# Attention and a wave mixer on one core: gates five loads deep, v copies on VectorE, x of batch 1 transposed by TensorE, padded v rows, a new issue order

## The chip, the cores and the metric

One core of one Trainium2 chip runs the whole program. The metric is the time of one execution in microseconds on the device, the median over runs. The span of a profile, from the first to the last instruction, is 1.7 to 1.8 us shorter than the time of the same execution. Only ratios from runs beside each other on one chip are compared closely.

## The reference, cut to what matters

```python
# q, k, v: (4 batches, 8 heads, 768, 64); each query sees 96 local keys and 8 global ones
scores = scale * q @ k^T + bias          # bias: -slope(head) * distance
a = softmax(where(keep, scores, -1e9))
x = (a @ v) as (4, 768, 512)
theta = x @ w_theta
y = w_tok_r @ (x * cos(theta)) + w_tok_i @ (x * sin(theta))   # over the 768 tokens
u = x + y
out = u + max(u @ w_ch, 0)
```

The kernel takes float32 inputs and computes in bf16. Each batch passes through attention in three groups `g` of 256 rows. The names in the profile are the tiles: `qk` (loaded q and k), `vn` (loaded v with a column of ones), `vp` (a copy of `vn` whose first 8 rows are the global rows), `e` (exponentials), `x`, `xT`, `zri` (x·cos, x·sin), `w_tokT`, `u`, `uT`.

## The kernel before

Every instruction is a named operation, issued in the order of one long string. Nothing is scheduled at run time: each engine takes its instructions in that order. The engine times and latencies handed to `add` are ignored here (`add` drops them), so the numbers in them change nothing on the chip.

```python
class Plan:
    def add(self, name, eng, fn, **_):
        op = self.ops[name] = SimpleNamespace(name=name, fn=fn, took=next(iter(eng)))
    def issue(self, order):              # "q000/DVE" sets the engine, then issues
        ...
DEPTH = 3
v_bufs  = [const.tile([T, 2, H, D + 1], BF, ...) for i in range(NV)]
vp_bufs = [const.tile([T, 2, H, D + 1], BF, ...) for i in range(NV)]

def load(fn, us, ndesc, spot, depth=0, ...):     # fn issues one DMA from GpSimd
    ...
    if depth:        # loads 24 to 86: a tiny GpSimd copy that reads load n-depth
        add(f"gate{n}", ..., lambda: nc.gpsimd.tensor_copy(out=scrap, in_=landed[n - depth]()), ...)
    add(f"load{n}", ..., fn, ...)

def vprev(b, g):     # vp: v with the global rows put in rows 0..7
    if b == 0:       # two VectorE copies, vpa and vpb
        ...
    else:            # two DMAs on the SP queue
        add(f"vpa{b}{g}", {"SP": 0.88}, lambda: nc.sync.dma_start(out=dst[NG:T], in_=src[NG:T]), ...)
        add(f"vpb{b}{g}", {"SP": 0.76}, lambda: nc.sync.dma_start(out=dst[0:NG]..., in_=first...), ...)

def xtrans(b, g):
    if b == 0:       # 8 TensorE transposes, then one copy xc out of PSUM
        ...
    else:            # one DMA transpose on the SP queue
        ...
```

A gate makes GpSimd wait until the load three places back has landed. So three of the gated loads are in flight at most. A q, k or v load moves 256 KB of float32 from HBM as 1024 pieces of 64 numbers.

The softmax here doesn't subtract the row's maximum and nothing guards it: scores larger than these inputs give would overflow.

Of the kernel before, what the change touches and what calls it, by code (L numbers as in the profile page):

```python
# [10 lines left out]
BF = mybir.dt.bfloat16  # L11
# [25 lines left out]
ones5 ones1 ones6 halfpi ones2 zero load1 ones3 ones0 ones4 warm0 load2 load3 rel load4 sid6 far0 sid2 far1  # L37
load5 dtab0 sid4 dtab1 dtab2 sid0 load6 sid3 sid1 sid5 sid7 ident dtab3 load7 t0001 etab6 bi0000 bi0001 bi0010
bi0011 etab3 load8 t0000 t0010 q000/DVE t0011 q001/ACT k000/DVE load9 k001/ACT kg000 load10 etab0 kg001 s001
etab5 load11 s000 t0100 x0000 load12 t0110 x0001 q010/DVE bi0020 x0010 bi0021 k010/DVE load13 s002 x0011  # L40
bi0030 etab1 bi0031 s003 load14 x0020 kg010 vpa00 x0021 bi0100 vpb00 load15 etab4 bi0101 s010 etab2 v002
load16 v000 v001 x0100 n000 x0101 load17 t0200 n002 x0030 q020/DVE x0031 load18 t0210 etab7 n001 bi0110 v003
load19 bi0111 k020/DVE s011 bi0120 load20 x0110 bi0121 s012 kg020 x0111 load21 n003 bi0130 x0120 vpa01 bi0131
load22 s013 x0121 vpb01 bi0200 load23 vpa02 x0130 xt00 vpb02 bi0201 x0131 v010 xc00/DVE v012 v013 n010 s020
v011 n012 x0200 bi0210 bi0211 n011 s021 x0201 bi0220 n013 x0210 bi0221 s022 x0211 xt01 x0220 gate24 bi0230
xc01/DVE bi0231 load24 x0221 v020 s023 n020 th000 gate25 x0230 load25 x0231 th010 cos000 gate26 load26 v023
th011 n023 gate27 v022 load27 sin000 tw11 n022 tw10 tw01 twc11/DVE gate28 twc10/ACT v021 load28 z000 th001
twc01/ACT n021 gate29 tw00 load29 cos001 xt02 twc00/DVE sin001 xc02/DVE cos010 gate30 load30 z001 sin010 th021
# [42 lines left out]
def kernel(  # L91
# [25 lines left out]

    bufs = dict(qk=6, qT=3, kk=3, e=8, x=8, xT=3, zri=5, cs=3, u=4, uT=3, o=3, w_nat=9, pa=4, pb=4)
# [4 lines left out]
    add = plan.add  # L123
    tiles = {}
# [531 lines left out]
```

## Time and profile before

| | before |
|---|---|
| time, median of 3 (range) | 204.88 us (203.74 to 206.62) |
| span of the profiled run | 203.4 us |
| TensorE busy | 172.8 us |
| VectorE / ScalarE busy | 127.2 / 100.1 us |
| TensorE idle in gaps over 0.15 us | 25.2 us |
| last load (86) lands at | 149.9 us |

The profiled run took 205.13 us and is labelled slow, which on one core only says that it is over 1.5% above the fastest run known of this kernel.

First, the page: busy time, and the span in 40 slices, where a digit is the busy share in tenths, and for `PEclk` the granted clock.

```profile
span 203.4 us, 3971 instructions
...
PE 172.8 (85%) x1532; PEld 91.7 (45%) x1532; DVE 127.2 (63%) x280; ACT 100.1 (49%) x175; POOL 84.9 (42%) x154
...
PE   7589789897949958898846998949999999999990
...
PEclk9999969999996999999987999997999999999997
```

TensorE (PE) is full in the last third and full of holes before it. The 6s and 7s of the clock row are windows of 3.4 us at half clock, four of them before the tail. The Trainium skill, "TensorE: Matmul & The Clock Gate", part 1, says that TensorE's clock is halved after an idle window of about 3.4 us and restored after a busy one; the trace agrees on the length of the windows (3.4 us each). What counts as idle it leaves open: TensorE's longest idle stretch in this run is 3.0 us, and the window at 27 us begins after a gap of 1.7 us.

The list of waits shows what ended TensorE's gaps: total us, times, longest.

```profile
PE pb L303 <- DMA w_nat<-in_moe_w_tok_r_dram: 5.7, 3, 2.5
PE pb L321 <- DMA qk<-in_q_dram: 5.6, 3, 2.6
PE pa L483 <- DMA xT<-x: 4.7, 3, 3.0
PE pb L321 <- DMA qk<-in_k_dram: 2.2, 2, 1.8
...
PE pa L440 <- DMA vp<-vn: 0.9, 2, 0.5
```

And what GpSimd (POOL) waited for in its gates, from the same view:

```profile
POOL scrap L207 <- DMA qk<-in_k_dram: 16.6, 13, 3.0
POOL scrap L207 <- DMA vn<-in_v_dram: 10.2, 9, 2.1
POOL scrap L207 <- DMA w_nat<-in_moe_w_tok_i_dram: 8.0, 2, 7.1
POOL scrap L207 <- DMA w_nat<-in_moe_w_tok_r_dram: 5.6, 3, 3.0
POOL scrap L207 <- DMA qk<-in_q_dram: 4.9, 8, 1.2
```

`scrap` is the output of a gate. The chain of waits (start, length, what) puts the two together; the gates and issues between these lines, under 1 us each, are left out:

```profile
69.36 6.00 DMA w_nat<-in_moe_w_tok_r_dram
75.95 3.68 DMA vn<-in_v_dram
80.20 5.15 DMA qk<-in_k_dram
85.92 5.57 DMA vn<-in_v_dram
92.06 6.19 DMA qk<-in_k_dram
98.82 3.57 DMA vn<-in_v_dram
...
104.35 7.18 DMA qk<-in_k_dram
111.57 0.40 PE pb L321 x4
```

Between 69 and 111 us the end of the program hangs on loads, each issued only when the one three back had landed.

### The profile page before, as it was taken

Reading aid. Unit: us, or ns where it says so; the run is one execution under the profiler, and the core shown is the slowest. Engines: PE = TensorE matmul, PEld = TensorE weight load, DVE = VectorE, ACT = ScalarE, POOL = GpSimd, SP = SyncE. Lnnn points to the kernel's source line nnn. Section 1 sums busy time; section 2 is a strip of 40 time slices with the busy share of each in tenths; the row PEclk is TensorE's granted clock in tenths of the full one; section 3 lists DMA queues with packets and bytes.
Section 4 is the critical chain, followed back from the end, with each engine's and each line's share of the span. In section 5 each row is a group of like instructions: output and inputs, shape, how many; then the busy total and the mean of one; then the engine's idle time right before and its main releaser. Section 6 shows DMA issues by size and latency. Waiting matters only on the chain.

```text
span 203.4 us, 3971 instructions
## 1 busy us (share of the span) xinstructions
PE 172.8 (85%) x1532; PEld 91.7 (45%) x1532; DVE 127.2 (63%) x280; ACT 100.1 (49%) x175; POOL 84.9 (42%) x154
## 2 busy tenths in 40 slices
PE   7589789897949958898846998949999999999990
PEld 1355446543624635534432554416464554444440
DVE  2467664875833857674643899525999786453341
ACT  2389748894204609566820777517944574210010
POOL 7999136624636537656562834536400000000000
PEclk9999969999996999999987999997999999999997
DMA  5999979998999999999999999999978375413433
GB/s 38 117 134 152 161 129 99 111 145 129 95 130 128 182 172 113 171 83 210 108 130 113 109 156 197 137 183 152 156 124 141 104 131 130 130 60 69 159 72 135
DMA packets 101323, 26.39 MB, mean 130 GB/s; under 512 B 94447, under 2 KB 97151, under 8 KB 101303
## 3 DMA queue, kind: packets, MB, share of 16 engines
q0 software_dynamic: 77664, 12.85, 87.0%
q1 hardware_dynamic: 23639, 13.28, 30.7%
q8 instruction: 12, 0.20, 0.4%
q14 instruction: 8, 0.07, 0.1%
HBM read 25.69 MB, written 6.29 MB: 157 GB/s over the span
## 4 chain that ended last, share of the span: by engine, by line
DMA 41%; PE 40%; POOL 11%; issue 4%; ACT 1%; DVE 0%; POOLq 0%
PE pb L525 19%; DMA qk<-in_k_dram 9%; PE pb L565 8%; DMA w_nat<-in_moe_w_tok_r_dram 8%; DMA vn<-in_v_dram 6%; POOL qk L220 6%; DMA xT<-x 6%; PE pa L483 5%; DMA w_nat<-in_moe_w_tok_i_dram 4%; DMA qk<-in_q_dram 4%; DMA w_ch_bf<-in_moe_w_ch_dram 4%; PE pa L388 3%; POOL vn L234 3%; PE pa L440 2%; PE pb L321 2%
## 5 line engine op out<-in xcount | busy, mean ns | idle before, releaser
L525 PE MATMUL pb<-zri,w_tokT 128*128 128x512 bf16 x288 | 71.8, 389 | 0.0
L411 ACT ACTIVATE e<-pa 128x512 bf16<-128x512 f32 (+1 forms) x96 | 46.7, 570 | 36.3 <-PE pa L388 36.0
L525 PEld LDWEIGHTS <-w_tokT 128*128 128x128 bf16 x288 | 26.7, 100 | 29.4 <-issue 2.8
L483 PE MATMUL pa<-w_theta_bf,xT 128*128 128x512 bf16 x96 | 24.6, 393 | 5.5 <-DMA xT<-x 4.7
L492 ACT ACTIVATE cs<-pa,halfpi 128x512 bf16<-128x512 f32 x24 | 16.6, 690 | 20.2 <-PE pa L483 20.2
L419 DVE TENSOR_TENSOR e<-e,etab 128x1024 bf16<-128x1024 bf16 (+1 forms) x36 | 22.4, 640 | 5.5 <-ACT e L411 5.5
L537 DVE TENSOR_TENSOR u<-x,pb 128x512 bf16<-128x512 bf16 x24 | 16.4, 684 | 13.6 <-PE pb L525 13.6
L565 PE MATMUL pb<-w_ch_bf,uT 128*128 128x512 bf16 x96 | 24.5, 380 | 0.0
L321 PE MATMUL pb<-ident,qk 128*128 128x128 bf16 x192 | 17.2, 243 | 8.1 <-DMA qk<-in_q_dram 5.6
L220 POOL DMA_DIRECT2D qk<-in_k_dram x24 | 22.1, 921 | 3.2 <-issue 2.9
L234 POOL DMA_DIRECT2D vn<-in_v_dram x24 | 21.2, 896 | 4.1 <-issue 4.1
L220 POOL DMA_DIRECT2D qk<-in_q_dram x24 | 21.3, 889 | 3.4 <-issue 2.0
L388 PE MATMUL pa<-qT,kk 64*128 64x128 bf16 x352 | 18.8, 230 | 2.0 <-ACT e L411 0.8
L504 DVE TENSOR_TENSOR zri<-x,cs 128x1024 bf16<-128x1024 bf16 x24 | 16.3, 686 | 6.5 <-ACT cs L494 6.3
L572 DVE SCALAR_TENSOR_TENSOR o<-pb,u 128x512 f32<-128x512 f32 x24 | 16.5, 686 | 5.9 <-PE pb L565 5.9
L321 PEld LDWEIGHTS <-qk 128*128 128x128 bf16 x192 | 14.1, 110 | 13.3 <-DMA qk<-in_q_dram 7.1
L440 PEld LDWEIGHTS <-e 128*128 128x128 bf16 x352 | 14.7, 98 | 9.1 <-issue 2.2
L333 DVE COPY kk<-pb 128x2048 bf16<-128x2048 bf16 (+1 forms) x12 | 14.1, 1175 | 7.1 <-PE pb L321 7.0
L388 PEld LDWEIGHTS <-kk 64*128 64x128 bf16 x352 | 11.1, 98 | 15.9 <-issue 10.1
L207 POOL COPY scrap<-qk 1x1 bf16<-1x1 bf16 x35 | 8.1, 231 | 21.7 <-DMA qk<-in_k_dram 16.6
L552 ACT COPY uT<-pb 128x512 bf16<-128x512 bf16 x5 | 2.9, 589 | 28.3 <-PE pb L548 28.3
L483 PEld LDWEIGHTS <-xT 128*128 128x128 bf16 x96 | 8.7, 100 | 16.3 <-DMA xT<-x 6.1
(57 smaller groups left out, 179.3 us busy)
## 6 DMA issues: line engine op xcount, KB each, us to landing
out_dram<-o SPq DMA_DIRECT2D x24, 256.0 KB, 3.6
qk<-in_q_dram POOLq DMA_DIRECT2D x24, 128.0 KB, 4.2
qk<-in_k_dram POOLq DMA_DIRECT2D x24, 128.0 KB, 4.8
vn<-in_v_dram POOLq DMA_DIRECT2D x24, 128.0 KB, 5.4
vp<-vn SPq DMA_DIRECT2D x9, 243.8 KB, 4.4
w_nat<-in_moe_w_tok_r_dram POOLq DMA_DIRECT2D x6, 192.0 KB, 6.5
w_nat<-in_moe_w_tok_i_dram POOLq DMA_DIRECT2D x6, 192.0 KB, 6.3
w_theta_bf<-in_moe_w_theta_dram POOLq DMA_DIRECT2D x1, 512.0 KB, 8.1
```

What stands on the lines that cost most here:

```text
L220: nc.gpsimd.dma_start(out=tiles[key][:, i, t].rearrange("p (h d) -> p h d", d=D), in_=(q, k)[i][b, :, r0:r0 + T, :].rearrange("h p d -> p ...
L234: nc.gpsimd.dma_start(out=v_bufs[i][:, t, :, 0:D], in_=v[b, :, r0:r0 + T, :].rearrange("h p d -> p h d"))
L321: nc.tensor.transpose(p_[:, t - u0, p], tiles[key][:, i, t, p * T:(p + 1) * T], ident)
L388: nc.tensor.matmul(p_[hh][:, s], lhsT=tiles["kk", b, kg][R, kt, p, r, :], rhs=tiles["qT", b, g][R, qt, p, :], start=not biased, stop=not b ...
L411: nc.scalar.activation(tiles[ek][:, hh, 0:n], tiles[pb[hh]][:, 0:n], AF.Exp, scale=scale)
L419: nc.vector.tensor_mul(e_[:, :, 0:n], e_[:, :, 0:n], etab[:, 2 * p:2 * p + 2, s0:s0 + n])
L440: nc.tensor.matmul(o, lhsT=l_, rhs=r_, start=(i == 0), stop=(i == len(mms) - 1))
L483: nc.tensor.matmul(p_, lhsT=tiles["xT", b, g][:, p, t, :], rhs=w_theta_bf[:, p, :], start=(p == 0), stop=(p == NP - 1))
L492: nc.scalar.activation(tiles[ck][:, 0], tiles[ps], AF.Sin, bias=halfpi)
L525: nc.tensor.matmul(p_, lhsT=w_tokT[wi][:, 2 * g + t, tt * T:(tt + 1) * T], rhs=tiles["z", b, g][:, t, wi, :], start=(n == 1 and t == 0 and ...
L565: nc.tensor.matmul(p_, lhsT=tiles["uT", b, tt][:, p, :], rhs=w_ch_bf[:, p, :], start=(p == 0), stop=(p == NP - 1))
L572: nc.vector.scalar_tensor_tensor(o_, in0=tiles[ps], scalar=0.0, in1=tiles[uk], op0=ALU.max, op1=ALU.add)
```

## The change

The intent, in its own words: v rows padded to 80 columns, copies of v with the global rows on VectorE and ScalarE, loads gated five deep, x of batches 0 and 1 transposed by TensorE, a new order.

```diff
-ones5 ones1 ones6 halfpi ones2 zero load1 ones3 ... (the whole order string)
+ones5 ones2 ones4 ones0 ones1 load1 zero ones3 ... (the whole order string; xc10, xc11, xc12 are new)
...
+    DP = 80
-    bufs = dict(qk=6, ..., o=3, w_nat=9, pa=4, pb=4)
+    bufs = dict(qk=6, ..., o=3, w_nat=7, pa=4, pb=4)
+    VP_ENG = (1,1,1,1)
+    X_PE = (1, 1, 0, 0)
+    U_PE = (1, 0, 0, 0)
-    DEPTH = 3
+    DEPTH = 5
-    v_bufs = [const.tile([T, 2, H, D + 1], BF, name=f"vn_{i}") for i in range(NV)]
+    v_bufs = [const.tile([T, 2, H, DP], BF, name=f"vn_{i}") for i in range(NV)]
...
-        if b == 0:
-            add(f"vpa{b}{g}", {"DVE": 0.36}, ...)
+        if VP_ENG[b]:
+            oa = add(f"vpa{b}{g}", dict(eng), lambda: rest(oa), ...)     # columns 0..64 only
+            ob = add(f"vpb{b}{g}", dict(eng), lambda: head(ob), ...)
         else:
             (the two SP DMAs, no longer reached)
...
-        if b == 0:            # in xtrans
+        if X_PE[b]:
```

The new order names no engine for `vpa` and `vpb`, so all of them run on VectorE and none on ScalarE.

More of the change, by code (lines that the diff above doesn't have):

```diff
@@ L36 @@
 ORDER = """
-ones5 ones1 ones6 halfpi ones2 zero load1 ones3 ones0 ones4 warm0 load2 load3 rel load4 sid6 far0 sid2 far1
-load5 dtab0 sid4 dtab1 dtab2 sid0 load6 sid3 sid1 sid5 sid7 ident dtab3 load7 t0001 etab6 bi0000 bi0001 bi0010
-bi0011 etab3 load8 t0000 t0010 q000/DVE t0011 q001/ACT k000/DVE load9 k001/ACT kg000 load10 etab0 kg001 s001
-etab5 load11 s000 t0100 x0000 load12 t0110 x0001 q010/DVE bi0020 x0010 bi0021 k010/DVE load13 s002 x0011
-bi0030 etab1 bi0031 s003 load14 x0020 kg010 vpa00 x0021 bi0100 vpb00 load15 etab4 bi0101 s010 etab2 v002
@@ L42 @@
-load16 v000 v001 x0100 n000 x0101 load17 t0200 n002 x0030 q020/DVE x0031 load18 t0210 etab7 n001 bi0110 v003
-load19 bi0111 k020/DVE s011 bi0120 load20 x0110 bi0121 s012 kg020 x0111 load21 n003 bi0130 x0120 vpa01 bi0131
-load22 s013 x0121 vpb01 bi0200 load23 vpa02 x0130 xt00 vpb02 bi0201 x0131 v010 xc00/DVE v012 v013 n010 s020
-v011 n012 x0200 bi0210 bi0211 n011 s021 x0201 bi0220 n013 x0210 bi0221 s022 x0211 xt01 x0220 gate24 bi0230
-xc01/DVE bi0231 load24 x0221 v020 s023 n020 th000 gate25 x0230 load25 x0231 th010 cos000 gate26 load26 v023
@@ L47 @@
-th011 n023 gate27 v022 load27 sin000 tw11 n022 tw10 tw01 twc11/DVE gate28 twc10/ACT v021 load28 z000 th001
-twc01/ACT n021 gate29 tw00 load29 cos001 xt02 twc00/DVE sin001 xc02/DVE cos010 gate30 load30 z001 sin010 th021
-cos011 gate31 z010 load31 t1000 sin011 th020 q100/DVE gate32 load32 z011 tw20 cos020 t1010 twc20/DVE sin020
-mx010 k100/DVE gate33 cos021 load33 mx011 sin021 gate34 kg100 vpa10 z020 load34 s100 s101 z021 x1000 vpb10
-mx000 x1001 x1010 m100 s102 x1011 mx001 x1020 m101 gate35 x1021 load35 s103 m102 mx002 x1030 gate36 x1031
@@ L52 @@
-load36 tw30 m103 mx012 twc30/ACT u00 gate37 v100 u01 load37 v102 v101 v103 n100 ut00 tw31 gate38 uc00/DVE
-load38 ut01 tw21 twc31/DVE uc01/ACT ch00 n101 gate39 twc21/ACT load39 n102 t1100 n103 mx030 q110/DVE gate40
-xt10 load40 mx031 o00 gate41 t1110 load41 st00 mx020 k110/DVE gate42 load42 tw40 mx022 kg110 twc40/DVE mx021
-gate43 s110 load43 u02 s111 x1100 mx032 gate44 x1101 load44 x1110 m110 s112 x1111 gate45 vpa11 u03 load45
-x1120 s113 m111 x1121 vpb11 tw41 ut03 x1130 gate46 twc41/DVE ch01 load46 uc03/ACT m112 x1131 ch03 gate47 o01
@@ L57 @@
-load47 m113 t1200 st01 mx040 o03 q120/ACT gate48 st03 v110 load48 v112 n110 v111 v113 gate49 t1210 n112 load49
-mx042 n111 gate50 k120/DVE load50 mx041 tw50 n113 ut02 twc50/DVE uc02/ACT gate51 xt11 load51 kg120 u04 s120
-s121 gate52 x1200 ch02 load52 x1201 vpa12 x1210 tw51 gate53 m120 load53 s122 x1211 vpb12 twc51/DVE ut04 x1220
-s123 uc04/DVE x1221 mx050 m121 gate54 x1230 m122 load54 th100 x1231 o02 gate55 mx052 load55 m123 cos100 st02
-mx051 gate56 load56 v120 u05 v122 sin100 v123 ch04 gate57 n120 load57 n123 v121 ut05 gate58 n121 th101 load58
@@ L62 @@
-uc05/ACT n122 ch05 cos101 z100 xt12 gate59 load59 sin101 o04 th111 z101 gate60 vpa20 th110 load60 o05 mx120
-vpb20 cos110 gate61 load61 st05 sin110 mx110 st04 cos111 z110 th120 sin111 gate62 z111 th121 load62 cos120
-sin120 t2010 cos121 t2000 k200/DVE gate63 mx111 load63 q200/ACT mx121 gate64 kg200 z120 sin121 load64 s200
-z121 s201 x2000 mx122 x2001 gate65 vpa21 x2010 load65 m200 x2011 s202 u12 vpb21 v200 x2020 gate66 mx112 n200
-load66 x2021 ut12 m201 t2100 gate67 u11 s203 load67 q210/ACT v201 m202 t2200 ut11 n201 x2030 t2110 x2031
@@ L67 @@
-q220/DVE v202 mx100 gate68 k210/DVE load68 mx102 gate69 kg210 load69 n202 t2210 s210 m203 s211 gate70 k220/DVE
-x2100 load70 mx101 x2101 x2110 v203 u10 ch11 gate71 vpa22 x2111 load71 m210 s212 vpb22 n203 gate72 mx140 x2120
-load72 kg220 ut10 m211 x2121 v210 s213 gate73 n210 load73 v211 x2130 mx141 xt20 o11 x2131 n211 s220 ch12 m213
-st11 x2200 gate74 load74 m212 x2201 v213 s221 n213 gate75 v212 load75 x2210 mx150 n212 x2211 m220 s222 xt21
-gate76 s223 load76 o12 x2220 mx151 x2230 m221 st12 x2221 v220 mx152 x2231 n220 m222 v221 gate77 th200 vpa30
@@ L72 @@
-load77 m223 n221 v222 vpb30 cos200 v223 gate78 ch10 load78 n222 n223 th210 o10 xt22 sin200 gate79 u15 mx142
-load79 z200 th201 ut15 u14 th211 cos201 ut14 gate80 sin201 load80 mx130 cos210 z201 st10 gate81 mx132 sin210
-load81 cos211 z210 mx131 sin211 th220 u13 gate82 load82 z211 th221 ut13 cos220 sin220 t3000 cos221 t3010
-q300/DVE gate83 vpa31 t3100 load83 sin221 k300/DVE ch15 q310/ACT vpb31 gate84 t3110 load84 kg300 o15 mx220
-k310/DVE gate85 st15 s300 load85 s301 x3000 t3200 kg310 x3001 z220 mx221 x3010 q320/DVE x3011 gate86 s302
@@ L77 @@
-load86 m301 s303 x3020 ch14 m300 x3021 z221 x3030 s310 x3031 o14 mx210 x3100 m302 st14 x3101 s311 m303 v302
-m310 v300 x3110 mx212 vpa32 x3111 n300 v310 n302 vpb32 v303 mx222 n310 n303 s312 u22 v301 x3120 mx211 n301
-x3121 ut22 t3210 u21 s313 k320/DVE ch13 xt30 x3130 x3131 mx200 o13 ut21 m312 mx201 m313 st13 v312 mx202 kg320
-n312 m311 s320 v313 u20 x3200 ch22 x3201 n313 ut20 mx250 o22 m320 s321 st22 s322 x3210 mx252 x3220 x3221 v320
-mx251 x3211 n320 m321 v311 s323 n311 th301 x3230 u25 xt31 x3231 th300 m322 m323 v321 cos300 v322 ut25 ch21
@@ L82 @@
-n321 n322 mx240 o21 sin300 mx242 st21 cos301 z300 mx241 sin301 z301 v323 th311 u24 ch25 n323 ut24 th310 o25
-xt32 ch20 cos310 sin310 mx230 st25 o20 cos311 z310 mx232 st20 sin311 z311 mx231 ch24 u23 th321 ut23 o24 th320
-st24 mx310 cos320 sin320 mx311 cos321 z320 ch23 sin321 z321 mx300 o23 mx312 st23 mx302 u31 mx301 ut31 mx320
-u30 mx322 ut30 mx321 ch31 u32 mx340 ut32 o31 ch30 st31 mx330 o30 mx341 st30 ch32 mx342 o32 mx331 st32 u34
-mx332 ut34 mx350 u33 mx352 ut33 mx351 ch34 u35 ut35 o34 ch33 uc35/ACT st34 ch35 o33 st33 o35 st35
+ones5 ones2 ones4 ones0 ones1 load1 zero ones3 halfpi ones6 warm0 load2 load3 rel load4 sid7 sid1 sid2 sid5
@@ new lines @@
+sid4 sid3 load5 far0 ident sid0 far1 t0000 load6 dtab0 t0010 q000/DVE k000/DVE load7 kg000 dtab1 dtab2 load8
+t0001 dtab3 sid6 etab2 bi0000 q001/DVE bi0001 bi0010 load9 t0011 etab6 bi0011 k001/DVE etab3 load10 kg001
+etab5 s000 load11 s001 x0000 x0010 bi0020 load12 t0100 x0011 etab1 q010/DVE t0110 load13 etab4 k010/DVE x0001
+load14 etab0 bi0021 s002 vpa00 load15 etab7 bi0030 kg010 bi0031 vpb00 s003 x0020 load16 v001 x0021 v000 bi0100
+x0030 n000 v002 load17 x0031 bi0101 bi0110 n001 s010 n002 load18 v003 bi0111 x0100 t0200 n003 x0101 t0210
@@ new lines @@
+load19 q020/DVE s011 load20 k020/DVE bi0120 x0110 bi0121 s012 load21 x0111 bi0130 vpa01 xt00 x0120 load22
+kg020 vpb01 bi0131 x0121 s013 load23 xc00/DVE v011 x0130 v010 bi0200 x0131 n010 bi0201 bi0210 s020 n011 v013
+x0200 vpa02 bi0211 s021 n013 x0201 bi0220 v012 vpb02 x0210 bi0221 n012 s022 x0211 gate24 v020 load24 x0220
+bi0230 n020 bi0231 v021 x0221 s023 gate25 n021 load25 v022 x0230 th000 n022 x0231 gate26 tw01 load26 cos000
+v023 twc01/DVE xt01 n023 gate27 tw00 load27 tw11 xc01/DVE xt02 sin000 twc00/DVE th001 gate28 twc11/ACT load28
@@ new lines @@
+xc02/DVE th011 z000 cos001 gate29 load29 sin001 th021 gate30 z001 load30 t1000 t1010 q100/DVE gate31 th010
+load31 k100/DVE tw20 cos010 gate32 tw10 load32 tw21 kg100 sin010 twc10/DVE th020 cos011 gate33 z010 load33
+sin011 mx010 twc20/DVE gate34 cos020 z011 load34 mx000 sin020 vpa10 gate35 cos021 mx001 z020 load35 sin021
+vpb10 mx011 twc21/DVE gate36 load36 z021 s100 s101 gate37 x1000 mx012 load37 x1001 x1010 m100 s102 x1011
+gate38 tw30 u01 x1020 load38 v100 mx002 x1021 n100 twc30/ACT gate39 m102 s103 load39 t1100 u00 x1030 gate40
@@ new lines @@
+mx020 x1031 q110/DVE load40 m103 ut00 gate41 mx022 load41 uc00/DVE m101 t1110 gate42 v101 load42 k110/DVE v103
+tw40 mx021 twc40/ACT gate43 n103 load43 v102 kg110 n101 gate44 n102 load44 s110 u02 s111 x1100 gate45 vpa11
+load45 x1110 xt10 vpb11 tw41 x1111 xc10/DVE ch00 gate46 x1101 load46 m111 twc41/ACT s112 m110 s113 gate47
+x1120 t1200 load47 o00 x1121 v110 gate48 q120/DVE ut02 x1130 st00 v111 load48 ut01 x1131 uc02/DVE tw31 m112
+gate49 uc01/ACT ch02 load49 m113 twc31/ACT t1210 o02 gate50 ch01 load50 k120/DVE st02 mx040 gate51 load51
@@ new lines @@
+kg120 n110 v112 mx041 n112 gate52 load52 n111 s120 mx042 o01 x1200 gate53 load53 x1201 vpa12 s121 st01 vpb12
+mx030 x1210 u04 gate54 load54 x1211 mx031 m120 m121 gate55 v120 load55 s122 n120 v121 x1220 ut04 gate56 n121
+v113 x1221 load56 mx032 n113 uc04/ACT m122 s123 gate57 load57 ch04 u03 x1230 x1231 v122 gate58 o04 xt11 load58
+th100 n122 xc11/ACT st04 gate59 m123 ut03 load59 th101 cos100 vpa20 vpb20 gate60 v123 uc03/DVE load60 th111
+n123 sin100 ch03 gate61 load61 cos101 z100 xt12 sin101 o03 gate62 th110 xc12/ACT load62 z101 st03 tw51 cos110
@@ new lines @@
+tw50 gate63 twc51/DVE th121 load63 sin110 twc50/DVE cos111 z110 t2010 gate64 sin111 load64 t2000 k200/DVE
+t2110 q200/ACT gate65 t2100 load65 th120 kg200 q210/DVE vpa21 gate66 k210/DVE s200 load66 cos120 mx050 sin120
+gate67 kg210 mx052 vpb21 cos121 load67 z111 sin121 t2200 z120 gate68 x2000 mx051 load68 x2001 q220/DVE s201
+m200 gate69 s202 u05 x2010 load69 t2210 x2020 z121 v200 x2021 ut05 gate70 mx110 x2011 uc05/DVE load70 k220/DVE
+mx112 gate71 load71 vpa22 s203 n200 ch05 x2030 gate72 m202 x2031 load72 s210 vpb22 v202 kg220 m201 x2100 mx111
@@ new lines @@
+gate73 n202 x2101 load73 v201 u11 mx120 gate74 n201 load74 ut11 s211 m203 mx122 x2110 m210 gate75 x2111 load75
+v203 o05 s212 v210 n203 gate76 x2120 mx121 st05 load76 n210 x2121 xt20 s213 u12 gate77 s220 x2130 load77 vpa30
+mx100 ut12 x2200 m212 gate78 x2201 mx101 vpb30 load78 x2131 m220 v212 s221 gate79 m213 load79 ch11 x2210 n212
+x2211 m211 v213 gate80 s222 load80 m221 v220 x2220 mx102 n213 gate81 x2221 load81 n220 mx140 u10 gate82 v221
+v211 load82 m222 ut10 s223 n221 mx141 x2230 o11 x2231 gate83 v222 mx142 load83 n211 st11 m223 xt21 th201
@@ new lines @@
+gate84 n222 load84 v223 vpa31 ch12 n223 gate85 load85 vpb31 mx150 xt22 o12 gate86 th200 u14 load86 st12 ch10
+ut14 cos200 mx151 o10 mx130 st10 sin200 cos201 mx132 z200 sin201 th210 z201 mx131 cos210 sin210 th211 u13 z210
+mx152 ut13 cos211 sin211 th221 u15 vpa32 t3110 ut15 vpb32 t3010 k310/DVE t3200 k300/ACT t3100 th220 q320/DVE
+q310/DVE t3210 cos220 kg300 t3000 kg310 k320/DVE sin220 ch14 cos221 ch13 z220 q300/ACT kg320 o14 mx200 sin221
+o13 st14 s300 z221 s301 st13 x3000 ch15 z211 x3001 x3010 m300 mx220 x3011 o15 mx202 m301 st15 mx201 mx221 u20
@@ new lines @@
+v300 ut20 s302 n300 v301 x3020 mx222 n301 x3021 s303 m302 s310 x3030 u22 mx210 x3031 x3100 ut22 m303 s311
+x3101 v302 mx211 x3110 m310 x3111 s312 n302 v303 m311 x3120 ch20 x3121 n303 s313 o20 v310 xt30 x3130 mx230
+n310 x3131 m312 v311 mx231 st20 m313 v312 n311 v313 ch22 n312 n313 s320 o22 mx212 xt31 x3200 x3201 s321 u21
+mx232 st22 x3210 m320 ut21 x3211 s322 u23 v320 x3220 mx250 n320 ut23 x3221 m321 s323 th300 m322 x3230 x3231
+th301 cos300 m323 v322 v321 n322 mx251 n321 sin300 ch21 cos301 z300 v323 sin301 mx240 o21 n323 mx242 st21 z301
@@ L87 @@
+xt32 mx241 th311 u24 th310 ut24 mx252 cos310 sin310 ch23 u25 cos311 z310 th320 ut25 sin311 o23 mx300 cos320
+z311 st23 sin320 th321 z320 ch24 cos321 sin321 mx310 o24 z321 mx301 st24 mx302 mx312 u30 mx311 ut30 ch25 u31
+mx320 ut31 o25 mx321 st25 mx322 ch30 u32 ch31 ut32 o30 mx330 o31 st30 mx340 st31 mx342 mx341 ch32 u34 mx331
+ut34 o32 mx332 st32 mx350 u33 mx351 ut33 mx352 ch34 u35 ut35 o34 ch33 uc35/ACT st34 ch35 o33 st33 o35 st35
 """
@@ L116 @@
     FAR = 1e6
-    bufs = dict(qk=6, qT=3, kk=3, e=8, x=8, xT=3, zri=5, cs=3, u=4, uT=3, o=3, w_nat=9, pa=4, pb=4)
+    bufs = dict(qk=6, qT=3, kk=3, e=8, x=8, xT=3, zri=5, cs=3, u=4, uT=3, o=3, w_nat=7, pa=4, pb=4)
     const = ctx.enter_context(tc.tile_pool(name="const", bufs=1))
@@ L147 @@
     BIASED = (0, 1, 2)
-    v_bufs = [const.tile([T, 2, H, D + 1], BF, name=f"vn_{i}") for i in range(NV)]
-    vp_bufs = [const.tile([T, 2, H, D + 1], BF, name=f"vp_{i}") for i in range(NV)]
+    v_bufs = [const.tile([T, 2, H, DP], BF, name=f"vn_{i}") for i in range(NV)]
+    vp_bufs = [const.tile([T, 2, H, DP], BF, name=f"vp_{i}") for i in range(NV)]
     w_theta_bf = const.tile([T, NP, DM], BF, name="w_theta_bf")
@@ L205, in load @@
         if depth:
-            add(f"gate{n}", {"POOL": 0.25},
+            add(f"gate{n}", {"POOL": 0.35},
                 lambda: nc.gpsimd.tensor_copy(out=scrap, in_=landed[n - depth]()),
@@ L210, in load @@
         add(f"load{n}", {"POOL": 0.62 + 0.00028 * ndesc}, fn, reads=reads, writes=list(writes) + [("ld", n)],
-            alloc=alloc, prio=-100 + n, lat=(1.05, us, 0.65), after=after)
+            alloc=alloc, prio=-100 + n, lat=(1.05, us + {2: 0.75, 3: 0.75, 17: 1.1}.get(n, 0.0), 0.65), after=after)
     def load_qk(b, g, i, t, depth=0):
@@ L235, in fn, with load_w @@
                                     in_=v[b, :, r0:r0 + T, :].rearrange("h p d -> p h d"))
-            load(fn, 0.87, T * H, lambda t=t: v_bufs[i][0:1, t, 0, 0:1], depth, reads=[("ones", i)],
+            load(fn, 0.92, T * H, lambda t=t: v_bufs[i][0:1, t, 0, 0:1], depth, reads=[("ones", i)],
                  writes=[("v", b, g)], alloc={("v", b, g): "v"} if t == 0 else None)
-    def load_w(key, dst, src, depth=0):
+    def load_w(key, dst, src, us, depth=0):
         load(lambda: nc.gpsimd.dma_start(out=dst, in_=src.rearrange("(c p) n -> p c n", p=T)),
-             2.54, 512, lambda: dst[0:1, 0, 0:1], depth, writes=[key])
+             us, 512, lambda: dst[0:1, 0, 0:1], depth, writes=[key])
     def load_w_tok(tt, depth=0):
@@ L247, in load_w_tok @@
                 out=new(key, "w_nat", [T, S], BF), in_=src[tt * T:(tt + 1) * T, :]),
-                0.97, 128, lambda key=key: tiles[key][0:1, 0:1], depth, writes=[key], alloc={key: "w_nat"})
+                0.95, 128, lambda key=key: tiles[key][0:1, 0:1], depth, writes=[key], alloc={key: "w_nat"})
     bufs["v"] = NV
@@ L258 @@
     load_v(0, 2)
-    load_w("w_theta", w_theta_bf, moe_w_theta)
+    load_w("w_theta", w_theta_bf, moe_w_theta, 1.88)
     def batch(b, g, part, depth=DEPTH):
@@ L273 @@
     batch(1, 0, 1)
-    load_w("w_ch", w_ch_bf, moe_w_ch, DEPTH)
+    load_w("w_ch", w_ch_bf, moe_w_ch, 2.05, DEPTH)
     load_w_tok(3, DEPTH)
@@ L349, in vprev, with cut, rest, head @@
         (src, dst), (src0, _) = vbuf(b, g), vbuf(b, 0)
-        first = src0[0:NG, 0:1]
         key = ("vp", b, g)
-        if b == 0:
-            add(f"vpa{b}{g}", {"DVE": 0.36}, lambda: nc.vector.tensor_copy(out=dst, in_=src),
-                reads=[("v", b, g)], writes=[key], alloc={key: "v2"})
-            add(f"vpb{b}{g}", {"DVE": 0.36},
-                lambda: nc.vector.tensor_copy(out=dst[0:NG], in_=first.to_broadcast([NG, 2, H, D + 1])),
-                reads=[("v", b, 0), key], writes=[key])
+        eng = {"DVE": 0.36, "ACT": 0.94} if VP_ENG[b] else None
+        def cut(a, n=D + 1):
+            return a[:, :, :, 0:n]
+        def rest(o):
+            vector[o.took](out=cut(dst), in_=cut(src))
+        def head(o):
+            vector[o.took](out=cut(dst[0:NG]), in_=cut(src0[0:NG, 0:1]).to_broadcast([NG, 2, H, D + 1]))
+        if VP_ENG[b]:
+            oa = add(f"vpa{b}{g}", dict(eng), lambda: rest(oa),
+                     reads=[("v", b, g)], writes=[key], alloc={key: "v2"})
+            ob = add(f"vpb{b}{g}", dict(eng), lambda: head(ob), reads=[("v", b, 0), key], writes=[key])
         else:
             add(f"vpa{b}{g}", {"SP": 0.88}, lambda: nc.sync.dma_start(out=dst[NG:T], in_=src[NG:T]),
-                reads=[("v", b, g)], writes=[key], alloc={key: "v2"}, lat=(0.9, 0.9, 0.6))
+                reads=[("v", b, g)], writes=[key], alloc={key: "v2"}, lat=(0.9, 1.3, 0.6))
             add(f"vpb{b}{g}", {"SP": 0.76},
@@ L363, in vprev @@
                     out=dst[0:NG].rearrange("p t h d -> p t (h d)"),
-                    in_=first.rearrange("p t h d -> p t (h d)").to_broadcast([NG, 2, H * (D + 1)])),
+                    in_=src0[0:NG, 0:1].rearrange("p t h d -> p t (h d)").to_broadcast([NG, 2, H * DP])),
                 reads=[("v", b, 0)], writes=[key], lat=(0.9, 0.1, 0.6))
@@ L433, in pe @@
                         s = 2 * t if g else 2 * t - 1
-                        mms = [(e_[:, hh, s], vbuf(b, (it - 1) // 2)[1][:, (it - 1) % 2, h, :]),
-                               (e_[:, hh, s + 1], vbuf(b, g)[0][:, t, h, :])]
+                        mms = [(e_[:, hh, s], vbuf(b, (it - 1) // 2)[1][:, (it - 1) % 2, h, 0:D + 1]),
+                               (e_[:, hh, s + 1], vbuf(b, g)[0][:, t, h, 0:D + 1])]
                     else:
-                        mms = [(e_[:, hh, 0], vbuf(b, g)[0][:, 0, h, :])]
+                        mms = [(e_[:, hh, 0], vbuf(b, g)[0][:, 0, h, 0:D + 1])]
                     o = o_[:, (2 * t + hh) * (D + 1):(2 * t + hh + 1) * (D + 1)]
@@ L474, in xtrans @@
                     in_=tiles[xk].rearrange("n p t c -> n (p t c)")),
-                reads=[xk], writes=[xt], alloc={xt: "xT"}, lat=(1.1, 1.3, -0.5))
+                reads=[xk], writes=[xt], alloc={xt: "xT"}, lat=(1.1, 1.7, -0.5))
     def theta(b, g, t):
@@ L512, in on_pe @@
     def on_pe(b, tt):
-        return b == 0 or (b == B - 1 and tt == NT - 1)
+        return U_PE[b] or (b == B - 1 and tt == NT - 1)
     done = {}
@@ L556, in mix @@
                 lambda: nc.sync.dma_start_transpose(out=new(ut, "uT", [T, NP, T], BF), in_=tiles[uk]),
-                reads=[uk], writes=[ut], alloc={ut: "uT"}, boost=40, lat=(1.1, 0.65, -0.5))
+                reads=[uk], writes=[ut], alloc={ut: "uT"}, boost=40, lat=(1.1, 1.0, -0.5))
     def chan(b, tt):
```

## The prediction

> **What bounds the kernel now.** TensorE is the engine to fill: busy 172.8 of 203.4 us (page, part 1). From 140 us on it never idles (windows: 10.00 of 10 us until 190). The loss is before: gaps on PE over 0.15 us sum to 25.2 us, about 21 after the first loads, and four windows of 3.4 us at half clock follow them (clock 0.83 to 0.85 in the windows at 20, 60, 100, 130 us), 1.7 us each, 6.8 together.
>
> Most gaps end with a DMA (waits, timeline): w_tok 1.06, 2.52, 2.09 us; q and k 0.43, 2.06, 0.98, 1.76; sum 10.9. DMA-transposed x: 1.08, 0.63, 2.96; sum 4.7. Copied v: 0.9. The chain of waits is 41% DMA; from 20 to 111 us mostly a ladder of load, gate, load.
>
> The gates set that pace. Loads 24 to 86 land between 30.3 and 149.9 us, 1.93 us each, at 5.2 us from issue to landing (medians 4.2 to 6.5 by kind, part 6). Three in flight give (5.2+0.6)/3 = 1.93, 0.6 being the gate and its wake-up. Before the gates start, loads 2 to 16 land every 1.03 us, so the DMA engines can go faster.
>
> **What the change does.**
> - Depth 5: pace (5.2+0.6)/5 = 1.16 us at unchanged latency; with queueing I estimate latency 6 to 7, pace 1.3 to 1.5. The 63 loads end near 112 us, not 150. In the new order load 86 stands after about 93 us of TensorE work, formerly 107 (0.86 us per four 512-column matmuls), so batch 3's transposes come 10 us of work after their loads.
> - v copies: 18 SP DMAs go. Despite the title the new order gives none to ScalarE: all 12 pairs run on VectorE, 9x0.42 + 9x0.42..0.77, about +8 us. With x copies and moved q copies DVE rises from 127 to about 139 us (9.83 of 10 us at 140 to 150 already).
> - x of batch 1 on PE: +1.3 us (3x0.45), minus three DMA transposes of 3.9 us and the 1.08 us gap. The 0.63 and 2.96 gaps are batch 2's and stay with DMA.
> - Rows of 80: copies keep 1040 elements, so 0.42 us; matmuls unchanged. Two fewer w_nat buffers: harmless.
>
> The Trainium skill, "DMA: Bandwidth & Descriptors", section "Issuing engines are not separate DMA queues", says all DMAs run on the same 16 engines; the trace agrees (loads took 5 to 6 us beside transposes and copies at 85 to 99 us, 3.5 when alone). So deeper loads lengthen x and u transposes; fewer SP copies repay that.
>
> **Sum.** Non-gap, non-throttled PE time 166 us, +1.3; start gaps 4.4; tail after PE 5; residual gaps, estimated, 7 to 8; one or two throttled windows 2 to 3: 187 to 188. I predict 188 us, range 181 to 198. Faster by over 2% 0.90, same 0.08, slower 0.02.
>
> **What would show it.** Loads 24 to 86 at 1.2 to 1.5 us each, last landing before 120 us; w_tok, q, k gaps on PE under 4 us in total; no vp DMA on SP; DVE near 139 us; one or two half-clock windows; chain mostly PE after 60 us.
>
> **What would make it wrong.** Latency of 8 to 9 us, keeping the pace at 1.7 and the time near 200; VectorE copies of v delaying exp products and so PE, or slowing POOL's issues; late DMA transposes of x in batches 2, 3; an order that exposes VectorE waits.

Four small slips in it: the mean time from issue to landing of loads 24 to 86 was 4.98 us, not 5.2; with the last landing at 149.9 us their pace was 1.90 us, 119.6 us over 63 loads; the sum was made of spans, so 1.7 us is missing from it; and "alone" in "3.5 when alone" means without copies and transposes beside them, but with other loads in flight (loads 24 to 30 took 3.5 to 4.2 us, those issued from 85 to 99 us mostly 4.8 to 6.2).

## The result, and the profile after

Ratios here are the mean time of one kernel's fast runs over the mean of the other's fast runs in the same rounds, so not quite the ratio of the medians that are quoted.

| | before | after |
|---|---|---|
| time, median of 3 (range) | 204.88 (203.74 to 206.62) | 181.48 (181.31 to 181.79) |
| ratio, 95% interval | | 0.885 (0.875 to 0.895) |
| span of the profile | 203.4 | 179.5 |
| TensorE busy / gaps over 0.15 us | 172.8 / 25.2 | 164.6 / 9.7 |
| VectorE / ScalarE busy | 127.2 / 100.1 | 136.3 / 100.2 |
| loads 24 to 86: pace, issue to landing | 1.90, 4.98 | 1.27, 5.17 |
| last load lands at | 149.9 | 109.5 |

The outputs are correct. On a second chip the same kernel had the ratio 0.904 (0.898 to 0.909); there before took 201.6 us and after 181.9 us. The gain is 11.5% on the one and 9.6% on the other.

The page of the kernel after:

```profile
span 179.5 us, 3986 instructions
...
PE 164.6 (92%) x1532; PEld 89.7 (50%) x1556; DVE 136.3 (76%) x303; ACT 100.2 (56%) x173; POOL 88.2 (49%) x154
...
PE   6488999998888989998999999999999999998991
...
PEclk9957999999999999999999999999999999999999
```

From the third slice to the last but one TensorE's row has no digit under 8, and the half clock is left only at the very start. The matmul count is as before although 24 transposes were added, while the weight loads rose by 24: the trace has lost 24 matmul records.

TensorE's waits after:

```profile
PE pb L325 <- DMA qk<-in_q_dram: 1.2, 3, 0.5
PE pa L400 <- ACT e L423: 0.9, 3, 0.4
...
PE pb L577 <- DMA uT<-u: 0.6, 1, 0.6
PE pb L307 <- DMA w_nat<-in_moe_w_tok_r_dram: 0.6, 1, 0.6
```

GpSimd's gates after:

```profile
POOL scrap L211 <- DMA w_theta_bf<-in_moe_w_theta_dram: 5.0, 1, 5.0
POOL scrap L211 <- DMA w_ch_bf<-in_moe_w_ch_dram: 2.0, 1, 2.0
...
POOL scrap L211 <- DMA qk<-in_k_dram: 0.9, 2, 0.6
...
POOL scrap L211 <- DMA vn<-in_v_dram: 0.7, 2, 0.5
...
POOL scrap L211 <- DMA qk<-in_q_dram: 0.2, 1, 0.2
```

The waits of a gate for a q, k or v load, 31.7 us before (16.6 + 10.2 + 4.9), are 1.8 us after. The chain of waits is made of TensorE's own work in the stretch that was a ladder of loads:

```profile
66.82 0.86 PE pb L537 x4
...
69.67 0.86 PE pa L495 x4
70.76 0.86 PE pa L495 x4
71.86 0.86 PE pa L495 x4
72.73 0.86 PE pb L577 x4
```

### The profile page after: what moved, and what is told of

Same layout as the page of the kernel before. It is cut to its first block, busy times and chain, and to the rows that moved or that the text cites. A ratio compares the mean times of both kernels' runs of the same rounds, so it can differ in the third digit from the quotient of the medians.

```text
span 179.5 us, 3986 instructions
## 1 busy us (share of the span) xinstructions
PE 164.6 (92%) x1532; PEld 89.7 (50%) x1556; DVE 136.3 (76%) x303; ACT 100.2 (56%) x173; POOL 88.2 (49%) x154
## 4 chain that ended last, share of the span: by engine, by line
PE 55%; DMA 16%; POOL 16%; issue 5%; ACT 2%; DVE 2%; POOLq 0%; DVEq 0%
PE pb L537 25%; PE pb L577 10%; PE pa L495 9%; POOL qk L224 8%; DMA w_theta_bf<-in_moe_w_theta_dram 4%; PE pa L452 4%; DMA w_ch_bf<-in_moe_w_ch_dram 4%; PE pa L400 4%; POOL vn L238 4%; POOL scrap L211 3%; DMA vn<-in_v_dram 3%; DMA w_nat<-in_moe_w_tok_i_dram 3%; PE pb L325 2%; DMA uT<-u 2%; POOL w_nat L250 1%
## 5 line engine op out<-in xcount | busy, mean ns | idle before, releaser
L537 PE MATMUL pb<-zri,w_tokT 128*128 128x512 bf16 x274 | 67.4, 379 | 1.0 <-issue 0.5
L423 ACT ACTIVATE e<-pa 128x512 bf16<-128x512 f32 (+1 forms) x96 | 47.5, 567 | 26.3 <-PE pa L400 25.8
L577 PE MATMUL pb<-w_ch_bf,uT 128*128 128x512 bf16 x91 | 23.8, 380 | 1.1 <-DMA uT<-u 0.6
L495 PE MATMUL pa<-w_theta_bf,xT 128*128 128x512 bf16 x91 | 23.6, 379 | 0.3
L224 POOL DMA_DIRECT2D qk<-in_k_dram x24 | 21.3, 886 | 1.9 <-DMA vn<-in_v_dram 1.0
L325 PE MATMUL pb<-ident,qk 128*128 128x128 bf16 x192 | 14.8, 229 | 2.5 <-DVE ident L175 1.2
L465 DVE TENSOR_TENSOR x<-pa,rec 128x256 bf16<-128x256 f32 x36 | 15.3, 424 | 1.2
L325 PEld LDWEIGHTS <-qk 128*128 128x128 bf16 x192 | 12.6, 103 | 6.9 <-DMA qk<-in_q_dram 2.6
L337 DVE COPY kk<-pb 128x2048 bf16<-128x2048 bf16 (+1 forms) x12 | 13.5, 1128 | 1.3 <-PE pb L325 1.3
L506 ACT ACTIVATE cs<-pa 128x512 bf16<-128x512 f32 x24 | 14.5, 604 | 0.0
L577 PEld LDWEIGHTS <-uT 128*128 128x128 bf16 x96 | 8.5, 98 | 10.1 <-DMA uT<-u 1.1
```

The source lines that it names most:

```text
L224: nc.gpsimd.dma_start(out=tiles[key][:, i, t].rearrange("p (h d) -> p h d", d=D), in_=(q, k)[i][b, :, r0:r0 + T, :].rearrange("h p d -> p ...
L325: nc.tensor.transpose(p_[:, t - u0, p], tiles[key][:, i, t, p * T:(p + 1) * T], ident)
L423: nc.scalar.activation(tiles[ek][:, hh, 0:n], tiles[pb[hh]][:, 0:n], AF.Exp, scale=scale)
L495: nc.tensor.matmul(p_, lhsT=tiles["xT", b, g][:, p, t, :], rhs=w_theta_bf[:, p, :], start=(p == 0), stop=(p == NP - 1))
L537: nc.tensor.matmul(p_, lhsT=w_tokT[wi][:, 2 * g + t, tt * T:(tt + 1) * T], rhs=tiles["z", b, g][:, t, wi, :], start=(n == 1 and t == 0 and ...
L577: nc.tensor.matmul(p_, lhsT=tiles["uT", b, tt][:, p, :], rhs=w_ch_bf[:, p, :], start=(p == 0), stop=(p == NP - 1))
```

## The experiments

The theory: the pace of the gated loads is the cause, and the depth of the gates sets it. The rivals: the new order does it, or the v copies that left the DMA queues do. In the labels, "new" is the changed kernel and "old" the kernel before, with the edit named. All twelve gave a correct result. "before" ran beside them at a median of 201.6, 201.6 and 202.8 us in the three sets (new_depth3 to new_vcopy_dma; new_again to new_depth8; the last four). The record's own verdict is "faster" for the four runs of the second set and "unclear" for the other eight, so the text goes by the intervals, and by ranges of single runs that lie apart: old_depth5 took 187.1 to 191.3 us, before beside it 200.2 to 203.8.

| label | time us | ratio to before (95%) | pace / latency of loads 24 to 86 | TensorE gaps on loads / xT / vp / uT, after 13 us |
|---|---|---|---|---|
| before | 204.9 | 1 | 1.90 / 4.98 | 10.9 / 4.7 / 0.9 / 0 |
| new_depth3 | 202.5 | 1.009 (1.003 to 1.015) | 1.75 / 4.46 | 10.5 / 0.6 / 0 / 0.3 |
| old_depth5 | 188.1 | 0.934 (0.927 to 0.942) | 1.40 / 5.85 | 0.4 / 2.8 / 1.8 / 2.1 |
| new_old_order | 183.7 | 0.915 (0.908 to 0.923) | 1.33 / 5.39 | 0 / 1.9 / 0 / 1.3 |
| new_vcopy_dma | 190.7 | 0.944 (0.933 to 0.955) | 1.33 / 5.57 | 0.3 / 0 / 6.4 / 1.5 |
| new_again | 181.9 | 0.904 (0.898 to 0.909) | 1.29 / 5.16 | 0.6 / 0 / 0 / 0.7 |
| new_rows65 | 180.7 | 0.900 (0.895 to 0.905) | 1.29 / 5.12 | 0.5 / 0 / 0 / 0.7 |
| new_x_dma | 185.2 | 0.920 (0.914 to 0.926) | 1.28 / 5.14 | 0 / 3.8 / 0 / 0 |
| new_depth8 | 180.1 | 0.895 (0.891 to 0.900) | 1.09 / 5.80 | 0 / 0 / 0 / 0.3 |
| new_depth3_vcopy_dma | 205.2 | 1.020 (1.012 to 1.028) | 1.75 / 4.50 | 4.5 / 2.2 / 6.8 / 2.4 |
| old_depth5_vcopy_dve | 187.1 | 0.928 (0.920 to 0.937) | 1.33 / 5.61 | 0.5 / 2.6 / 0 / 1.0 |
| new_vcopy_act | 187.4 | 0.933 (0.926 to 0.940) | 1.16 / 4.75 | 0 / 0 / 0 / 0.5 |
| new_ungated | 180.8 | 0.898 (0.892 to 0.904) | 0.95 / 7.27 | 0 / 0 / 0 / 0.6 |

Latency is the mean from issue to landing (in old_depth5, of the 55 loads whose landing the trace gives), pace the time from load 23's landing to load 86's over 63.

### The depth, undone and alone

```diff
 (the changed kernel: new_depth3)
-    DEPTH = 5
+    DEPTH = 3
```

> The changed kernel with the gates back at three deep, nothing else. Theory (the pace of the gated loads is the main cause): loads 24 to 86 return to about 1.7 to 1.9 us each, last landing near 140 us, stalls of TensorE on loads come back, time 196 to 204 us. Rival order (the new order is what matters, the depth is not): time stays within 184 us. Rival copies (taking the v copies off the DMA queues is what made loads quick): pace about 1.4 us even at depth three, time 183 to 188 us.

Measured: 202.5 us, the pace 1.75 us, the last load at 137.7 us, stalls on loads 10.5 us. The whole gain is gone. Both rivals, as stated, are refuted: neither the new order nor the quick copies help when the gates are three deep.

Two lists of waits of this run show a second effect. VectorE's:

```profile
DVE u L549 <- PE pb L537: 18.7, 15, 3.0
DVE vp L361 <- DMA vn<-in_v_dram: 14.5, 7, 4.2
```

and TensorE's:

```profile
PE pa L452 <- DVE e L431: 8.0, 4, 3.7
PE pb L325 <- DMA qk<-in_q_dram: 4.7, 6, 1.7
PE pb L307 <- DMA w_nat<-in_moe_w_tok_r_dram: 3.2, 3, 1.6
PE pb L325 <- DMA qk<-in_k_dram: 2.6, 2, 1.6
```

A copy of v on VectorE waits for its v load in VectorE's own queue, 14.5 us in all, and the products of exponentials behind it come late for TensorE (8.0 us). At five deep (the kernel after) such waits are 0.8 us in all.

```diff
 (the kernel before: old_depth5)
-    DEPTH = 3
+    DEPTH = 5
```

> The kernel before with gates five deep, nothing else. Theory: loads 24 to 86 at 1.3 to 1.5 us each, the 10.9 us of load stalls mostly go, but the order puts load 86 behind 107 us of TensorE work and keeps DMA copies and transposes, so 188 to 194 us. Rival order: within 2% of before (201 to 208 us). Rival copies: loads queue behind the v copies, pace no better than 1.7 us, time 198 to 205 us.

Measured: 188.1 us, 6.6% under before, from one digit changed. The pace is 1.40 us and the stalls on loads are 0.4 us past the start. What is left are stalls on transposed x and u and on copied v, 6.7 us together, all of them DMAs on the SP queue:

```profile
PE pa L483 <- DMA xT<-x: 2.8, 2, 1.8
...
PE pb L565 <- DMA uT<-u: 2.1, 1, 2.1
PE pa L440 <- DMA vp<-vn: 1.8, 1, 1.8
```

Depth alone is about two thirds of the gain (13.5 of the 19.7 us between the medians 201.6 and 181.9).

### The order

```diff
 (the changed kernel: new_old_order)
-ORDER = (the new string)
+ORDER = (the old string, with xc10/ACT, xc11/ACT, xc12/ACT put behind xt10, xt11, xt12)
```

> The changed kernel in the old order (three tokens for the copies of batch 1's transposed x added on ScalarE), all other parts new. Theory: loads are as quick as the order lets them be, 184 to 190 us. Rival order: close to before, 197 to 205 us, since only the order is missing.

Measured: 183.7 us, just below the range expected. Both sets saw before at 201.6 us, and there the new order is worth 183.7 to 181.9 us, about 1%; the intervals of the two ratios (0.908 to 0.923 and 0.898 to 0.909) overlap by a hair, so even this 1% is not quite settled.

### The v copies

```diff
 (the changed kernel: new_vcopy_dma)
-    VP_ENG = (1,1,1,1)
+    VP_ENG = (1,0,0,0)
-    DP = 80
+    DP = 65
```

> The changed kernel with the v copies of batches 1 to 3 back as DMAs on the SP queue (rows of 65 again, since the pad is never written), order as new. Theory: 2.3 MB more on the DMA engines lengthen the loads to about 5.7 us, pace 1.4, and the copies' 4.4 us latency delays some value products; VectorE loses 8 us of work that was not limiting; time 183 to 188 us. Rival copies: back above 193 us, with load latency 6.5 us or more.

Measured: 190.7 us, above what the theory expected and below what the rival did. The loads slow down as expected (latency 5.57 us, pace 1.33 us), but TensorE waits for the copies themselves, in its list of waits:

```profile
PE pa L452 <- DMA vp<-vn: 6.4, 3, 4.0
```

and two windows at half clock come back in mid-kernel (6.8 and 3.4 us). The six copies whose landing the trace gives took 3.8 to 8.5 us from issue to landing here, 5.4 at the median. (Before, the trace gives only two, issued after the 140th us, 4.0 and 4.7 us.) The new order was made for copies of half a microsecond. So this run overstates what the part is worth; the next one asks the same in the old order.

```diff
 (the kernel before: old_depth5_vcopy_dve)
-    DEPTH = 3
+    DEPTH = 5
-        if b == 0:             # in vprev
+        if True:
```

> The kernel before with gates five deep and all v copies on VectorE, old order, rows of 65, x of batch 1 still transposed by DMA. Theory: load latency falls from 5.85 us to about 5.3 us, TensorE stalls on copied v (1.8 us) and on transposed x and u (4.9 us) shrink by half; ratio to before 0.91 to 0.925, against 0.934 of old_depth5 and 0.915 of new_old_order. Rival (the copies only pay in the new order): ratio 0.93 or more.

Measured: ratio 0.928, between the two expectations. The stalls on copied v are gone and the pace falls to 1.33 us, but the interval overlaps that of old_depth5 (0.934): in the old order the part is worth under 2%, and its size is not settled. Load latency fell to 5.61 us, not 5.3, and the stalls on transposed x and u from 4.9 to 3.7 us, not by half.

```diff
 (the changed kernel: new_depth3_vcopy_dma)
-    DEPTH = 5
+    DEPTH = 3
-    VP_ENG = (1,1,1,1)
+    VP_ENG = (1,0,0,0)
-    DP = 80
+    DP = 65
```

> The changed kernel with gates three deep and, as well, the v copies of batches 1 to 3 back as DMAs (rows of 65). Theory (at three deep the other parts of the change gain nothing because the VectorE copies of v put the wait for a v load into VectorE's queue: 14.5 us of such waits in new_depth3, and 8.0 us of TensorE stalls on VectorE's exp products behind them): the VectorE waits on v loads fall under 3 us, the TensorE stalls on exp products under 3 us, but latency rises by 0.5 us to about 5.0 us (pace 1.85 to 1.95) and stalls on copied v come; load pace and so the time is about that of new_depth3, 198 to 206 us. Rival (the VectorE copies are what holds new_depth3 back, the pace is not): 195 us or less.

Measured: 205.2 us, as the theory had it, though the pace stayed at 1.75 us and the latency at 4.50 us, both lower than expected. No wait of VectorE on v loads is left in its list past the start, and no stall of TensorE on the products over 0.2 us. In their place TensorE waits for the DMA copies:

```profile
PE pa L452 <- DMA vp<-vn: 6.8, 3, 3.8
PE pb L307 <- DMA w_nat<-in_moe_w_tok_r_dram: 2.7, 2, 1.9
PE pb L577 <- DMA uT<-u: 2.4, 2, 1.6
```

This fits VectorE's queue being only the place where the late loads showed in new_depth3: moving the copies off it moves the wait, and the time does not fall. But the copies as DMAs bring a wait of their own (those the trace gives took 3.5 to 5.1 us), so the run does not separate the two.

```diff
 (the changed kernel: new_vcopy_act, in the order string)
-vpa10 ... vpb10 ... (18 names of batches 1 to 3)
+vpa10/ACT ... vpb10/ACT ...
```

> The changed kernel with the v copies of batches 1 to 3 on ScalarE instead of VectorE, as the change's own words have it; order otherwise the same. Theory (VectorE, near 9 of 10 us busy from 50 to 100 us, is close to limiting there, ScalarE has room on average, but a ScalarE copy takes about 1 us, so 18 us more): VectorE falls to 128 us, ScalarE rises to 117 us, its exponentials wait behind the copies; time within 1.5% of new_again, no gain over 1%. Rival (VectorE's copies cost TensorE time): 1% or more faster than new_again's 0.904.

Measured: ratio 0.933, 3% slower than new_again, more than expected. VectorE was busy 129.8 us and ScalarE 116.7, as expected. One copy takes 1.08 us on ScalarE and 0.43 us on VectorE, in the view of the tile `vp`, whose columns give shortest, median and longest in ns:

```profile
L361 ACT COPY vp<-vn x9: 1067/1079/1114, 40.7 to 121.9; 128x1040 bf16<-128x1040 bf16 x9
L361 DVE COPY vp<-vn x3: 430/430/783, 16.2 to 26.6; 128x1040 bf16<-128x1040 bf16 x3
```

The exponentials wait behind the copies on ScalarE, and TensorE behind the exponentials (4.3 us against 0.9 us in the kernel after):

```profile
PE pa L400 <- ACT e L423: 4.3, 8, 1.5
```

The loads were even quicker here (1.16 us; the gates took 224 ns in the mean, against 307 in new_again), so load pace is no longer what limits the kernel after. The engine that the change's title names but its order does not use is the wrong one, in this order.

### x of batch 1

```diff
 (the changed kernel: new_x_dma)
-    X_PE = (1, 1, 0, 0)
+    X_PE = (1, 0, 0, 0)
-xc10/DVE ... xc11/ACT ... xc12/ACT   (in the order string)
```

> The changed kernel with the transposes of x of batch 1 back on DMA (the three TensorE transposes and their three copies left out of the order). Theory: TensorE saves 1.3 us of work, but three DMA transposes of about 6 us land late beside the deeper loads: stalls of TensorE on transposed x of 2 to 6 us return, load latency up 0.2 us; time 1 to 3% above new_again. Rival (this part is not worth its TensorE time): equal to or faster than new_again.

Measured: ratio 0.920 against 0.904, so 1.8% slower. Stalls on transposed x of 3.8 us return, as expected, and one half-clock window of 3.4 us; the latency of the loads does not rise (5.14 us). The DMA transposes of x take 4.1 us at the median here, up to 6.1; those of batch 1, beside the loads, 5.2 to 6.0. Eight TensorE transposes cost 0.45 us and are worth it.

### The padded rows

```diff
 (the changed kernel: new_rows65)
-    DP = 80
+    DP = 65
```

> The changed kernel with v rows of 65 columns instead of 80. Theory (the padding does little): within 1% of new_again; v loads' latency within 0.3 us of new_again's; the VectorE copy of v 0.42 to 0.44 us either way. Rival (the 32-byte aligned rows make v loads land sooner): v loads take over 0.5 us longer than q and k loads do, the pace of loads 24 to 86 rises from 1.27 to 1.35 us or more, and the time by 1 to 2%.

Measured: the same time (0.900 against 0.904, the intervals overlap) and the same pace. The rival is half right about the loads: a v load takes 5.2 us at the median, against 4.6 in new_again, while q and k loads take 4.3 and 4.4 here. Nothing waits for those 0.6 us. The padding is worth nothing that these runs can see.

### The yardstick, and deeper gates

> The changed kernel once more, unedited, as the yardstick for the runs beside it on this chip: ratio to before 0.88 to 0.895.

Measured: 0.904, outside the range, because before was quicker on this chip (201.6 against 204.9 us) and the kernel after was not.

```diff
 (the changed kernel: new_depth8)
-    DEPTH = 5
+    DEPTH = 8
```

> The changed kernel with gates eight deep. Theory (at five the loads are already out of TensorE's way; 1.4 us of TensorE stalls on loads are left): pace 1.05 to 1.15 us, latency 7 to 8 us, load stalls under 1 us, time within 1% of new_again, gain at most 1.5 us. Rival (the pace is still the limit at five): 2% or more faster. Third possibility (deeper queue delays the DMA transposes of x and u): stalls on them over 3 us and 1% or more slower.

Measured: 180.1 us, 0.9% under new_again, no stall on loads left. The pace was 1.09 us as expected, but the latency only 5.80 us, not 7 to 8.

```diff
 (the changed kernel: new_ungated)
-    DEPTH = 5
+    DEPTH = 0
-gate24 ... gate86   (in the order string)
```

> The changed kernel with no gates at all (the 63 gate copies left out); loads are held only by buffers coming free. Theory: pace about 1.0 us, set by POOL's issue of 0.88 us and by the DMA engines; latency 8 us or more; no TensorE stalls on loads; the deeper queue delays w_tok, and DMA transposes run later without loads beside them; within 1% of new_depth8's 0.895. Rival (gates protect the DMA transposes and stores): stalls on transposed x and u over 3 us and ratio above 0.91.

Measured: 0.898, the same as new_depth8 within the intervals. The loads come every 0.95 us with 7.27 us of latency, the last at 88.6 us. That is about 7.6 in flight (7.27 / 0.95). The gates protect nothing in this kernel: the DMA transposes of x come after the loads are done and land in 3.0 to 3.1 us, where in the kernel after batch 2's, beside the loads, took 5.5 to 7.5. Both versions beat before by 10%, and the kernel after by at most 1%, which the intervals do not quite settle.

## Why the prediction was right, point by point

The time, 181.5 us, lies in the range (181 to 198) but at its low end, 6.5 us under the 188 predicted, and 8 us under it with the 1.7 us of the third slip put in. The range of 17 us was wide enough to hold that.

**The cause was right.** The prediction put the loss to the gates' pace. Undone, the depth takes the whole gain back (1.009); alone, it gives 6.6%. The four other parts and the two buffers fewer give nothing without it and about 3% with it, from 0.934 to 0.904. The run new_depth3 shows why they don't simply add. Its loads end 12 us sooner than before (137.7 against 149.9 us), but the new order leaves more work behind the last load: 64 us to the end of the span, against 53 us before. The order assumes quick loads. That this is why the two cancel is argued from these times, not shown by a run of its own.

**The pace: nearly the right number, partly for the wrong reason, and so partly by luck.** I expected 1.3 to 1.5 us from (latency + 0.6)/5 with latency rising to 6 or 7 us. Measured: 1.27 us at 5.17 us. The formula would then give 1.15 us. What mostly sets the pace at five deep is GpSimd itself: from the issue of load 24 to that of load 86 (78 us) it is busy 68.7 us, with 52.6 us of issuing loads and 18.8 us of gates, which overlap a little, and waits only 5.9 us for a landing, where before it waited 41.6 of 118 us. The run new_depth8 fits: GpSimd is busy 67.5 of 71.8 us there, and 5.0 of the 6.2 us saved are its idle time. That the latency hardly grows because GpSimd, as the brake, keeps the DMA engines from queueing up is argued, not shown.

**The gates were slower than assumed.** A gate takes 214 ns in the mean before and 301 ns after. The timelines of GpSimd and of VectorE in new_again show one of the slow ones (start, length, engine, what):

```profile
53.86 1.31 POOL L211 COPY scrap<-qk 1x1 bf16<-1x1 bf16 x1
```

```profile
53.85 1.27 DVE L431 TENSOR_TENSOR e<-e,etab 128x1024 bf16<-128x1024 bf16 x2
```

The copy of one element lasts as long as two products on VectorE and ends 0.05 us after them; all 17 gates over 0.25 us of that run overlap a product of two SBUF tiles, or a copy between SBUF tiles, on VectorE, and each ends 34 to 49 ns after the end of such an instruction; of the 46 shorter gates 14 overlap one. The Trainium skill, "SBUF — State Buffer", section "Who interferes with whom", says that a VectorE instruction with two SBUF inputs shares a port with GpSimd's reads, and that whichever starts first has it to itself. The trace agrees. It adds that one gate can sit behind two products in a row. The prediction had named VectorE's copies of v slowing GpSimd's issues as a risk: the issues kept their 0.9 us, the gates became slower.

**The sum.** Its terms in us of span:

| term | predicted | measured |
|---|---|---|
| TensorE between gaps, at full clock | 167.3 | 162.7 |
| gaps at the start (to 13 us) | 4.4 | 4.4 |
| later gaps | 7 to 8 | 5.3 |
| loss at half clock | 2 to 3 | 3.4 |
| after TensorE's last matmul | 5 | 3.7 |
| sum | 187 | 179.5 |

Measured, the first row is 175.8 us (end of the last matmul) less 9.7 us of gaps less half of the 6.8 us at half clock. The mis-sized term is the first: time "between gaps" is not all work. The profile draws a 512-column matmul 380 ns long, but the next one can start 216 ns after it; a stall behind such a matmul shows 164 ns too short, or not at all. The usual distances from one start to the next (216 ns behind 512 columns, and 56, 37 and 29 ns behind the three small kinds) add up to an estimated 151 us for all matmuls before, and 152 us after with the lost records counted. That leaves 15 us of the first row before (166 us), and 10 us after: time behind matmuls that shows as no gap. I had counted the 15 us as work that stays, and by this estimate 5 of them went away with the stalls. This rests on charging the half clock in full; if it cost nothing (next paragraph), 14 us are left after, and the half clock is the more mis-sized term.

**The half clock.** The window after the change lies at 8.7 to 15.5 us. It cost little or nothing: the three runs had mean clocks of 0.981, 0.958 and 1.000 and took 181.31, 181.79 and 181.48 us. Charging it in the table is therefore an upper bound.

**The rest.** VectorE's 139 us were 136.3; that all v copies went to it was read right from the order. Stalls of TensorE on loads were 1.4 us (under 4 predicted). The feared late transposes of x did not come: no stall on them in the kernel after. The three that ran beside loads did take longer, as predicted (5.5 to 7.5 us, against 3.0 to 3.1 for the other three), but the new order does not need them sooner.

**What stays open.** The separate worth of the order (about 1%), of the v copies (0.7% in the old order with overlapping intervals, 4% in the new one) and of depth eight over five (0.9%). The two w_nat buffers were not tried alone.

## What to carry to other kernels

When a chain of waits is a ladder of transfer, gate, transfer, divide the latency by the number in flight before looking at bandwidth: two more in flight were worth more here than all the reordering. Then look for the next brake on that path, which here was the issuing engine and not the DMA engines. Parts of a change that were tuned together are worth what they are worth only together: the other parts of this change, made for quick loads, gained nothing on slow ones, and moving a copy to another engine moves its wait into that engine's queue.

## What the Trainium skill lacked or had wrong

- "DMA: Bandwidth & Descriptors": it has no figure for what a load costs the issuing GpSimd when it has many pieces. Its table of where a DMA's fixed time goes calls the making of descriptors small and variable. Here GpSimd was busy 0.89 to 0.91 us per q, k or v load of 1024 pieces (means after the change), against 0.58 us for a w_tok load of 128 rows (mean before); at five in flight this, with the gates, kept it busy 69 of 78 us.
- The same page gives no figure for DMA transposes beside many small loads. Here a transpose of x landed in 5.5 to 7.5 us beside loads five deep, and in 3.0 to 3.1 us when the loads were over.
- "SBUF — State Buffer", "Who interferes with whom", says that the blocked engine waits for the whole instruction. Here a one-element GpSimd copy waited through two VectorE products in a row (1.31 us against 0.18 when free).
- "TensorE: Matmul & The Clock Gate" is right on the length of the window (3.4 us). Its Terms give the penalty as throttled time times the missing share of the clock, which would be 3.4 us for the 6.8 us at half clock at the start of the kernel after; the run with that window took 181.31 us and one at full clock throughout 181.48 us.
